# Sliding-window attention feeding an FFN: scores packed into full PSUM banks across units, sink scores of four units in one column-tiled group

## The chip, the cores and the metric

The kernel runs on one core of one Trainium2 chip. The metric is the device time of one execution in microseconds (us). Of the kernel before there are three runs: 232.1, 232.37 and 232.55 us, median 232.37.

## The reference

```python
batch, n_heads, seq, head_dim = (4, 8, 768, 64)
n_sink, window = (4, 128)
n_tokens, d_model, d_ff = (3072, 512, 2048)

def _attn_ref(q, k, v, n_sink, window):
    scale = 1.0 / np.sqrt(D)
    scores = scale * np.matmul(q, k.transpose(0, 1, 3, 2))
    is_sink = pos[None, :] < int(n_sink)
    rel = pos[:, None] - pos[None, :]
    in_window = (rel >= 0) & (rel < int(window))
    scores = np.where(is_sink | in_window, scores, -1000000000.0)
    a = softmax(scores)
    return np.matmul(a, v)

def _moe_ref(x, w_in, w_out, beta):
    h = x @ w_in
    g = h * (1.0 / (1.0 + np.exp(-beta * h)))
    return g @ w_out
```

The attention output, transposed to tokens by 512 (heads x 64), is the x of the feed-forward part. Inputs and output are float32. A query sees the 128 keys of its window and the first 4 keys of its sequence, the sinks. In blocks of 128 that is its own block (the diagonal, "d"), the block before (the upper part, "p"), and for queries from block 2 on the four sinks as well. Query blocks 0 and 1 contain or touch the sinks in key block 0 ("s").

## The kernel before, in words

**Units.** The work of attention is cut into 32 units: a batch (4), half of its sequence (384 queries), and a pair of heads. Unit u is batch u // 8, half u // 4 % 2, pair u % 4. Four units make a half batch, called hb in the code (0 to 7), even ones the first half of a sequence, odd ones the second. The FFN runs on the same 384 tokens of a half batch, T_.

**Stages.** Each is a small function that records its operations in a graph (`Graph.add`):

- `load`, `cast`: q, k, v from HBM (SP queue) into float32 staging and then to bf16. v goes to `vaug` with a column of ones, which yields the softmax denominator.
- `T` (units of hb 0 to 2) and `XP` (later ones): transposed q and k, `qkT`, head pair in the 128 partitions, 64 each. `T` does it on TensorE, `XP` by DMA.
- `SC` (L609 to L653): scores of one unit, keys in the partitions. Each head uses 64 rows of the array. It takes four neighbouring PSUM banks of 512 float32 columns: two groups of blocks (`GROUPS`, L597), and for each group one bank a head. The first half of a sequence has groups of 3 and 2 blocks, the second half 3 and 3, so banks are filled to 384 or 256 columns of 512. An exponential on ACT for each group (L639) writes `E`, and GpSimd masks the "d" and "p" blocks (L645); the "s" blocks are multiplied by `maskS` (L651).
- `SS` (L655 to L667): sink scores of one unit. `kS` holds the 4 sink keys of each head, zero elsewhere, in columns 0 to 3 and 32 to 35 of 128. One matmul of 128x128 weights (L662) and one exponential (L665) into `ES`. `first_keys` (L550) fills `kS`, and two copies from `vaug` (L543) fill `vS`, the sink values.
- `AV` (L681 to L711): for each of three query blocks the sink product (L691, one matmul for both heads) and the window products (L701); then a reciprocal and a multiplication on VectorE (L705, L707) give `onorm`.
- `OT`: `onorm` transposed to `xT`, on TensorE (L727) for the first units, later by DMA.
- `HQ` (L745): 4 matmuls of 384 columns for one of 16 chunks of the hidden layer; tanh on ACT (L750) and one VectorE operation (L752) give `g`. `OQ` (L765): 4 matmuls of 512 columns, one of four parts of a 128-token output; after the fourth it is copied and stored.

**What sets the order.** The main loop at the end of `_program` keeps a planned clock, and at each step takes the first stage, in the order OT, AV, SC, SS, T and then alternately HQ and OQ, whose inputs and PSUM banks are ready by the plan (`head`, L796). The attention of later half batches is so spread among the FFN of earlier ones. `Graph.arrange` then orders all operations again, with planned durations, may swap neighbouring groups of TensorE, and chooses ACT, VectorE or GpSimd for copies that any of them can do. `resolve` sets the semaphore waits. Banks are taken with `take(n)`: n neighbouring banks that come free first. Up to 18 us matmuls on constants (L935) fill the gaps of TensorE.

Rings that bound how far stages run ahead: `NE` = 4 units of `E` and `ES`, `NKS` = 4 of `kS`, `NON` = 5 of `onorm`, `NTT` = 3 of the tanh output.

Of the kernel before, what the change touches and what calls it, by code (L numbers as in the profile page):

```python
# [347 lines left out]
def _program(nc, G, sb, ps, q, k, v, w_in, w_out, beta, out):  # L348
    NU = 2 * NPAIR
    NSTG, NX, NV, NT, NE, NON, NG, NTT, NOS, NKS, NWS = 2, 2, 3, 12, 4, 5, 3, 3, 4, 4, 6  # L350
# [22 lines left out]
    E = sb("E", (128, 6, 2, 128), BF16, NE)  # L373
    ES = sb("ES", (128, HALF), BF16, NE)
    kS = sb("kS", (128, 128), BF16, NKS)
    vS = sb("vS", (128, H, D + 1), BF16, 2)
    onorm = sb("onorm", (128, NK, 2, D), BF16, NON)
# [45 lines left out]
    def banks_at(n):  # L423
        c = choose(n)
        return c and c[0]
# [23 lines left out]
    def consts():  # L449
# [11 lines left out]
        for i in range(NKS):  # L461
            add("gp", lambda e, i=i: e.memset(kS[i][:, :], 0.0), 80, w=[("kS", i)])
        for i in range(2):
            add("gp", lambda e, i=i: e.memset(vS[i][:, :, :], 0.0), 350, w=[("vS", i)])
# [54 lines left out]
    def cast(hb, n, i):  # L519
# [18 lines left out]
        if n == "v" and hb % 2 == 0 and i == 0:  # L538
            z = hb // 2 % 2
            v0 = vaug[hb % NV][0:NSINK, 0, :, :].rearrange("p (a two) d -> p a two d", two=2)  # L540
            for hh in range(2):
                dst_ = vS[z][32 * hh:32 * hh + NSINK, :, :].rearrange("p (a two) d -> p a two d", two=2)[:, :, hh, :]
                add("dve", lambda e, dst_=dst_, hh=hh: e.tensor_copy(dst_, v0[:, :, hh, :]), 200,  # L543
                    r=[("vS", z), ("v", hb % NV, 0)], w=[("vSd", z, hh)])
# [5 lines left out]
    def first_keys(u):  # L550

        ks = u % NKS
        kd = kS[ks][:, :].rearrange("p (a w) -> p a w", w=32)[:, 0:2, 0:NSINK]
        add("gp", lambda e: e.tensor_tensor(
            kd, qkT[:, u % NT, 1:2, 0:NSINK].to_broadcast([128, 2, NSINK]),
            headm[:, :].unsqueeze(2).to_broadcast([128, 2, NSINK]), ALU.mult), 200,
            r=[("kS", ks), ("qkT", u % NT, 1, 0), "headm0", "headm"], w=[("kSd", ks)])

    def XP(hb, n, c):
# [9 lines left out]
        if hb % 2 == 0 and (n, c) == ("k", 0):  # L569
            for j in range(4):  # L570
                first_keys(4 * hb + j)

    def T(u):
# [16 lines left out]
        if hb % 2 == 0:  # L590
            first_keys(u)
# [5 lines left out]
    GROUPS = [[[("s", 0, 0), ("s", 0, 1), ("d", 1, 1)], [("d", 2, 2), ("p", 1, 2)]],  # L597
              [[("d", 3, 3), ("p", 2, 3), ("p", 3, 4)], [("d", 4, 4), ("d", 5, 5), ("p", 4, 5)]]]

    def slots(half):  # L600

        out_, i = {}, 0
        for j, grp in enumerate(GROUPS[half]):
            for blk in grp:
                out_[blk] = (j, i)
                i += 1
        return out_

    def SC(u):  # L609
        G.begin()  # L610
        b, half, hp = where(u)
        z = u % NE
        bs = take(4)
        for j, grp in enumerate(GROUPS[half]):

            jobs = {}
            for i, (kind, kb, qb) in enumerate(grp):
                jobs.setdefault(kb, []).append((qb, i))
            for kb, cols in jobs.items():
                cols.sort()  # L620
                own = u if kb >= NK * half else u - 4
                kt = qkT[:, own % NT, 1, :]
# [3 lines left out]
                for hh in range(2):  # L626
# [3 lines left out]
                    add("pe", lambda e, dst=dst, kt=kt, kc=kc, rows=rows, q0=q0, nq=nq: e.matmul(  # L630
                        dst, kt[rows, kc:kc + 128],
                        qkT[rows, u % NT, 0, q0:q0 + 128 * nq].rearrange("p (s w) -> p s w", w=128),
                        start=True, stop=True), mm_ns(128 * nq) / 2 + 24,
                        r=qk_keys(u) + (qk_keys(own) if own != u else []), x=[("B", bs[2 * j + hh])])
        for j, grp in enumerate(GROUPS[half]):
            n, s0 = len(grp), slots(half)[grp[0]][1]
            src = P[:, bs[2 * j]:bs[2 * j] + 2, 0:128 * n].rearrange("p h (s w) -> p h s w", w=128)
            dst_ = E[z][:, s0:s0 + n, :, :].rearrange("p s h w -> p h s w")
            add("act", lambda e, src=src, dst_=dst_: e.activation(dst_, src, AF.Exp, bias=0.0, scale=SCALE),  # L639
                act_ns(256 * n), w=[(k_, z, j) for k_ in "Edps"], x=[("B", i) for i in bs[2 * j:2 * j + 2]])  # L640
            for kind, sg in (("d", 1), ("p", -1)):
                at_ = [i for i, blk in enumerate(grp) if blk[0] == kind]
                if at_:
                    d = E[z][:, s0 + at_[0]:s0 + at_[-1] + 1, :, :].rearrange("p s h w -> p (s h) w")
                    add("gp", lambda e, d=d, sg=sg, at_=at_: e.affine_select(  # L645
                        d, d, [[0, 2 * len(at_)], [sg, 128]], ALU.is_ge, 0.0, base=min(sg, 0), channel_multiplier=-sg),
                        pool_ns(256 * len(at_), 2 * len(at_)), r=[("E", z, j)], w=[(kind, z, j)])
            if grp[0][0] == "s":
                d = E[z][:, s0:s0 + 2, :, :]
                mask = maskS[:, :, :].unsqueeze(2).to_broadcast([128, 2, 2, 128])  # L650
                fn = lambda e, d=d, mask=mask: e.tensor_tensor(d, d, mask, ALU.mult)  # L651
                any_of({"gp": (fn, 1150), "dve": (fn, 335)}, r=[("E", z, j), "maskS"], w=[("s", z, j)])
        give(bs)  # L653

    def SS(u):  # L655

        G.begin()
        b, half, hp = where(u)
        z, ks = u % NE, (u - 4 * half) % NKS
        q0 = 0 if half else 256  # L660
        bs = take(1)
        add("pe", lambda e: e.matmul(P[:, bs[0], q0:HALF], kS[ks][:, :], qkT[:, u % NT, 0, q0:HALF], start=True,  # L662
                                     stop=True), mm_ns(HALF - q0),
            r=[("kSd", ks)] + qk_keys(u), x=[("B", bs[0])])
        add("act", lambda e: e.activation(ES[z][:, q0:HALF], P[:, bs[0], q0:HALF], AF.Exp, bias=0.0, scale=SCALE),  # L665
            act_ns(HALF - q0), w=[("ES", z)], x=[("B", bs[0])])
        give(bs)  # L667

    def parts(half):

        sl = slots(half)
        return [[(blk[0], sl[blk][0], sl[blk][1], blk[1])
                 for blk in sorted(sl, key=lambda x: "spd".index(x[0])) if blk[2] == qb]
                for qb in range(NK * half, NK * half + NK)]

    def av_keys(u):
        z = u % NE
        ks = {(p[0], z, p[1]) for ps in parts(where(u)[1]) for p in ps}
        return sorted(ks) + [("v", u // 4 % NV, c) for c in range(NK)] + [("ES", z), ("vSd", u // 8 % 2, 1)]

    def AV(u):  # L681
        G.begin()
        b, half, hp = where(u)
        z, on = u % NE, u % NON
        bs = take(1)
        A = P[:, bs[0], :]
        for m, ps in enumerate(parts(half)):
            far = NK * half + m >= 2
            if far:
                c0 = 2 * m * (D + 1)  # L690
# [105 lines left out]
    def head(s):  # L796
# [10 lines left out]
        elif s in ("SC", "SS"):  # L807
            if i >= NU or i >= done["AV"] + NE:
                return None
# [192 lines left out]
```

The softmax here doesn't subtract the row's maximum and nothing guards it: scores larger than these inputs give would overflow.

## Time and profile before

| | |
|---|---|
| time, median of three | 232.37 us |
| span of the profiled execution | 230.6 us |
| TensorE (PE) busy | 216.6 us, 94% |
| ScalarE (ACT) busy | 156.6 us, 68% |
| VectorE (DVE) busy | 135.0 us, 59% |
| GpSimd (POOL) busy | 73.3 us, 32% |
| DMA queue of the loads and stores | 72.7% of 16 engines' span |

How to read the profile: section 2 of its page cuts the span into 40 slices of 5.77 us, a digit is the busy share in tenths. A row of a group gives line, engine, operation, output and inputs, shapes, count, then busy us and mean ns of one, then the idle time of the engine before it and what ended it. A row of the timeline gives start, duration, engine, line, operation and how many; the durations of matmuls overlap, so the distance of two starts says how long PE was held. PEld is the weight load.

### The profile page before, as it was taken

What the parts mean: (1) busy time and instruction counts of PE and PEld (TensorE: products, weight loads), DVE (VectorE), ACT (ScalarE), POOL (GpSimd) and SP (SyncE); (2) the same over time, 40 slices, a digit from 0 to 9 for tenths busy, and PEclk for the clock granted to TensorE, in tenths of its full rate; (3) what the DMA queues carried; (4) which work ended last, traced back from release to release, by engine and by line L of the source; (5) the groups of instructions that cost most, each with busy time, mean ns of one, the idle gap of its engine ahead of it and who ended that gap; (6) DMA issues with size and microseconds to landing.
All of it is one profiled execution on the core that took longest, in us unless ns stands there. A gap on an engine that the chain in (4) does not pass through costs nothing.

```text
span 230.6 us, 4557 instructions
## 1 busy us (share of the span) xinstructions
PE 216.6 (94%) x1730; PEld 122.0 (53%) x1756; DVE 135.0 (59%) x285; ACT 156.6 (68%) x282; POOL 73.3 (32%) x163
## 2 busy tenths in 40 slices
PE   7986899899999999999998999999999999999993
PEld 5563555356555555555554455645554665555541
DVE  3895698987783567747574554836665453633310
ACT  2867979487882986686777776867769754744431
POOL 6583953022361572153001493225002730000000
PEclk9999999999999999999999999999999999999999
DMA  5999999999859988899439979997587022011112
GB/s 159 249 325 261 296 388 387 356 247 223 128 126 241 209 113 163 216 189 162 92 96 251 218 106 204 259 170 134 87 185 219 20 80 64 3 45 45 45 50 89
DMA packets 94997, 39.76 MB, mean 172 GB/s; under 512 B 81648, under 2 KB 87808, under 8 KB 94976
## 3 DMA queue, kind: packets, MB, share of 16 engines
q1 hardware_dynamic: 94976, 39.47, 72.7%
q8 instruction: 14, 0.23, 0.4%
q14 instruction: 7, 0.06, 0.1%
HBM read 27.27 MB, written 6.29 MB: 146 GB/s over the span
## 4 chain that ended last, share of the span: by engine, by line
PE 76%; DMA 10%; ACT 4%; SPq 4%; DVE 2%; issue 1%; POOL 1%
PE P L765 34%; PE P L745 30%; DMA wst<-in_moe_w_in_dram 4%; PE P L630 4%; DMA k_stage<-in_k_dram 4%; SPq L499 4%; PE P L701 4%; DMA v_stage<-in_v_dram 2%; DVE g L752 1%; ACT t L750 1%; PE P L691 1%; ACT qkT L439 1%; ACT E L639 1%; PE P L662 1%; PE P L581 1%
## 5 line engine op out<-in xcount | busy, mean ns | idle before, releaser
L752 DVE SCALAR_TENSOR_TENSOR g<-t,P 128x384 bf16<-128x384 f32 x128 | 69.6, 552 | 49.3 <-ACT t L750 45.6
L750 ACT ACTIVATE t<-P,hbeta 128x384 f32<-128x384 f32 x128 | 73.6, 588 | 35.0 <-PE P L745 28.6
L745 PE MATMUL P<-xT,w_in 128*128 128x384 bf16 x512 | 96.3, 326 | 0.9 <-DVE w_in L444 0.3
L765 PE MATMUL P<-w_out,g 128*128 128x512 bf16 x358 | 91.8, 379 | 2.7 <-DVE g L752 1.3
L645 POOL TENSOR_SCALAR_AFFINE_SELECT E<-E 128x512 bf16<-128x512 bf16 (+1 forms) x112 | 55.2, 522 | 66.7 <-ACT E L639 66.1
L745 PEld LDWEIGHTS P<-xT,w_in 128*128 128x128 bf16 x512 | 48.1, 98 | 37.6 <-DVE g L752 0.9
L765 PEld LDWEIGHTS P<-w_out,g 128*128 128x128 bf16 x384 | 35.6, 98 | 37.1 <-DVE g L752 2.8
L639 ACT ACTIVATE E<-P 128x768 bf16<-128x768 f32 x64 | 45.6, 770 | 7.5 <-PE P L630 7.3
L439 ACT ACTIVATE osb<-P 128x512 f32<-128x512 f32 x20 | 12.0, 599 | 12.7 <-PE P L765 11.2
L701 PE MATMUL P<-vaug,E 128*128 128x65 bf16 x352 | 18.9, 193 | 0.7 <-DVE vaug L444 0.7
L701 PEld LDWEIGHTS P<-vaug,E 128*128 128x128 bf16 x352 | 16.7, 97 | 4.2 <-DVE vaug L444 0.9
L707 DVE TENSOR_TENSOR onorm<-P,rden 128x384 bf16<-128x384 f32 x32 | 17.8, 557 | 1.0
L630 PE MATMUL P<-qkT 64*128 64x128 bf16 (+1 forms) x256 | 16.1, 239 | 1.0 <-ACT E L639 0.9
L630 PEld LDWEIGHTS P<-qkT 64*128 64x128 bf16 x256 | 8.6, 94 | 11.3 <-issue 5.0
L444 DVE CAST q<-q_stage 128x512 bf16<-128x512 f32 (+1 forms) x17 | 9.0, 540 | 7.0 <-DMA q_stage<-in_q_dram 7.0
L691 PE MATMUL P<-vS,ES 128*128 128x130 bf16 x64 | 12.8, 220 | 0.0
L444 DVE CAST vaug<-v_stage 128x512 bf16<-128x512 f32 x16 | 7.3, 456 | 8.2 <-DMA v_stage<-in_v_dram 8.1
L665 ACT ACTIVATE ES<-P 128x128 bf16<-128x128 f32 (+1 forms) x32 | 10.9, 410 | 0.4 <-PE P L662 0.4
L441 POOL TENSOR_SCALAR_AFFINE_SELECT vaug<-v_stage 128x512 bf16<-128x512 f32 x3 | 2.1, 693 | 25.5 <-DMA v_stage<-in_v_dram 25.5
L651 DVE TENSOR_TENSOR E<-E,maskS 128x512 bf16<-128x512 bf16 x15 | 7.0, 463 | 5.0 <-ACT E L639 4.8
L444 DVE CAST k<-k_stage 128x512 bf16<-128x512 f32 (+1 forms) x14 | 6.5, 464 | 5.7 <-DMA k_stage<-in_k_dram 5.5
L935 PE MATMUL P<-ones 128*128 128x256 bf16 x47 | 8.7, 322 | 1.1 <-POOL ones L450 1.1
(50 smaller groups left out, 107.1 us busy)
## 6 DMA issues: line engine op xcount, KB each, us to landing
v_stage<-in_v_dram SPq DMA_DIRECT2D x24, 256.0 KB, 4.6
out_dram<-osb SPq DMA_DIRECT2D x24, 256.0 KB, 2.4
q_stage<-in_q_dram SPq DMA_DIRECT2D x15, 256.0 KB, 4.9
k_stage<-in_k_dram SPq DMA_DIRECT2D x15, 256.0 KB, 4.9
wst<-in_moe_w_in_dram SPq DMA_DIRECT2D x5, 512.0 KB, 9.1
wst<-in_moe_w_out_dram SPq DMA_DIRECT2D x4, 512.0 KB, 6.8
g<-in_moe_w_out_dram SPq DMA_DIRECT2D x4, 512.0 KB, 7.1
q_stage<-in_q_dram SPq DMA_DIRECT2D x2, 768.0 KB, 7.2
```

What stands on the lines that cost most here:

```text
L439: return lambda e: e.activation(dst, src, AF.Copy, bias=0.0, scale=scale)
L444: return lambda e: e.tensor_copy(dst, src)
L630: add("pe", lambda e, dst=dst, kt=kt, kc=kc, rows=rows, q0=q0, nq=nq: e.matmul(dst, kt[rows, kc:kc + 128], qkT[rows, u % NT, 0, q0:q0 + 12 ...
L639: add("act", lambda e, src=src, dst_=dst_: e.activation(dst_, src, AF.Exp, bias=0.0, scale=SCALE), act_ns(256 * n), w=[(k_, z, j) for k_ i ...
L645: add("gp", lambda e, d=d, sg=sg, at_=at_: e.affine_select(d, d, [[0, 2 * len(at_)], [sg, 128]], ALU.is_ge, 0.0, base=min(sg, 0), channel_ ...
L691: add("pe", lambda e, m=m, c0=c0: e.matmul(A[:, c0:c0 + 2 * (D + 1)], ES[z][:, m * 128:(m + 1) * 128], vS[b % 2][:, 2 * hp:2 * hp + 2, :]. ...
L701: e.matmul(A[:, c0:c0 + D + 1], E[z][:, i, hh, :], vaug[vz][:, kb % NK, 2 * hp + hh, :], start=a, stop=o, skip_group_check=True), 39,
L707: add("dve", lambda e: e.tensor_tensor(onorm[on][:, :, :, :].rearrange("p m h d -> p (m h) d"), av[:, :, 0:D], rden[on][:, :].unsqueeze(2) ...
L745: add("pe", lambda e, c=c: e.matmul(hp, w_in16[:, c, m * 128:(m + 1) * 128], xT[:, c, t0:t0 + HALF], start=(c == 0), stop=(c == 3)), mm_ns ...
L750: add("act", lambda e: e.activation(tt[ti][:, :], hp, AF.Tanh, bias=0.0, scale=hbeta[:, m:m + 1]), act_ns(HALF) + 93, r=["hbeta"], w=[("t" ...
L752: add("dve", lambda e: e.scalar_tensor_tensor(gt[T_ % NG][:, m, :], tt[ti][:, :], 1.0, hp, ALU.add, ALU.mult), dve_ns(HALF), r=[("t", ti)] ...
L765: add("pe", lambda e, m=m: e.matmul(P[:, bk, :], gt[T_ % NG][:, m, t * 128:(t + 1) * 128], w_out16[:, m, :], start=(m == 0), stop=(m == NM ...
```

## The change

It repacks the scores and merges the sink scores.

- **Tiles instead of groups.** `tiles_of` lists tiles of exactly four blocks, each in one bank a head, so 512 of 512 columns. In an even half batch each unit fills one tile with s, s, d, d, and the four "p" blocks of the four units share a fifth tile. In an odd half batch two units share three tiles. `E` becomes a ring of 7 tiles, and blocks that a later AV needs are found through `PLACE`.
- **Bursts.** `SC(n)` now does burst n: two tiles (one in half batch 0), four banks at once. There are three bursts for each half batch after the first (six a batch, for eight before).
- **Sinks in one group.** `SS` is no stage of its own. It runs inside the last burst of an even half batch and inside the first of an odd one, for the four units together: four matmuls of 32 weight columns, each to 32 partitions of the same bank, and one exponential. `kS` keeps the four units side by side, 32 columns each.
- **Sink values by DMA.** `vS` must now hold head h in partitions 16 h to 16 h + 3. Four small DMAs (`load_first`) bring the first four values of all batches and heads into `vS32`, and one VectorE multiplication a batch by a 0/1 table `own` spreads them (`first_values`), in place of the two copies.
- **Masks.** All masks on GpSimd are of two blocks and two heads, 512 columns.
- The planner's conditions follow: scores of a unit are counted as done when the last burst that holds a block of it is done (`units_scored`).

The core of the diff:

```diff
-    NSTG, NX, NV, NT, NE, NON, NG, NTT, NOS, NKS, NWS = 2, 2, 3, 12, 4, 5, 3, 3, 4, 4, 6
+    NSTG, NX, NV, NT, NE, NON, NG, NTT, NOS, NWS = 2, 2, 3, 12, 7, 5, 3, 3, 4, 6
...
-    E = sb("E", (128, 6, 2, 128), BF16, NE)
-    ES = sb("ES", (128, HALF), BF16, NE)
-    kS = sb("kS", (128, 128), BF16, NKS)
+    E = sb("E", (128, 4, 2, 128), BF16, NE)
+    ES = sb("ES", (128, HALF), BF16, 2)
+    kS = sb("kS", (128, 128), BF16, 2)
...
+    def load_first(s_):
+
+        add("sp", lambda e: e.dma_start(vS32[s_:128:16, :, :], v[:, :, s_, :].rearrange("b h d -> h b d")), 60,
+            r=["vS32z"], w=[("vS32", s_)], dma=f"ds{s_}")
+
+    def first_values(b):
+
+        z = b % 2
+        add("dve", lambda e: e.tensor_tensor(
+            vS[z][:, :, 0:D], vS32[:, b:b + 1, :].to_broadcast([128, H, D]),
+            own[:, :].unsqueeze(2).to_broadcast([128, H, D]), ALU.mult), dve_ns(H * D),
+            r=[("vS32", s_) for s_ in range(NSINK)] + ["own", ("vSo", z)], w=[("vS", z)])
...
-    GROUPS = [[[("s", 0, 0), ("s", 0, 1), ("d", 1, 1)], [("d", 2, 2), ("p", 1, 2)]],
-              [[("d", 3, 3), ("p", 2, 3), ("p", 3, 4)], [("d", 4, 4), ("d", 5, 5), ("p", 4, 5)]]]
...
+    def tiles_of(hb):
+
+        u = 4 * hb
+        if hb % 2 == 0:
+            return [[("s", u + i, 0, 0), ("s", u + i, 0, 1), ("d", u + i, 1, 1), ("d", u + i, 2, 2)]
+                    for i in range(4)] + [[("p", u + i, 1, 2) for i in range(4)]]
+        out_ = []
+        for a in (u, u + 2):
+            b_ = a + 1
+            out_ += [[("d", a, 3, 3), ("d", a, 4, 4), ("p", a, 2, 3), ("p", a, 3, 4)],
+                     [("d", a, 5, 5), ("d", b_, 3, 3), ("p", a, 4, 5), ("p", b_, 2, 3)],
+                     [("d", b_, 4, 4), ("d", b_, 5, 5), ("p", b_, 3, 4), ("p", b_, 4, 5)]]
         return out_
...
+        step = 1 if hb_ == 0 else 2
+        runs_ = [list(range(i, min(i + step, first + n_))) for i in range(first, first + n_, step)]
+        with_first = len(runs_) - 1 if hb_ % 2 == 0 else 0
+        BURSTS += [(r_, hb_ if i == with_first else None) for i, r_ in enumerate(runs_)]
...
+    def SC(n):
         G.begin()
-        b, half, hp = where(u)
-        z = u % NE
-        bs = take(4)
-        for j, grp in enumerate(GROUPS[half]):
+        tiles, first = BURSTS[n]
+        bs = take(2 * len(tiles))
+        f_ = take(1) if first is not None else None
+        for j, t_ in enumerate(tiles):
...
+        if first is not None:
+            SS(first, f_[0])
...
-                act_ns(256 * n), w=[(k_, z, j) for k_ in "Edps"], x=[("B", i) for i in bs[2 * j:2 * j + 2]])
...
+                act_ns(1024), w=[("E", z)] + [("m", z, i) for i in range(4)],
+                x=[("B", i) for i in bs[2 * j:2 * j + 2]])
...
-        add("pe", lambda e: e.matmul(P[:, bs[0], q0:HALF], kS[ks][:, :], qkT[:, u % NT, 0, q0:HALF], start=True,
-                                     stop=True), mm_ns(HALF - q0),
-            r=[("kSd", ks)] + qk_keys(u), x=[("B", bs[0])])
...
+    def SS(hb, bank):
+
+        ks, z = hb // 2 % 2, hb % 2
+        q0 = 0 if hb % 2 else 256
+        for j in range(4):
+            u = 4 * hb + j
+            add("pe", lambda e, j=j, u=u: e.matmul(
+                P[32 * j:32 * j + 32, bank, q0:HALF], kS[ks][:, 32 * j:32 * j + 32], qkT[:, u % NT, 0, q0:HALF],
+                start=True, stop=True), 100 if j == 0 else (mm_ns(HALF - q0) if j == 3 else 5),
+                r=[("kSd", ks, j)] + qk_keys(u), x=[("B", bank)])
+        add("act", lambda e: e.activation(ES[z][:, q0:HALF], P[:, bank, q0:HALF], AF.Exp, bias=0.0, scale=SCALE),
+            act_ns(HALF - q0), w=[("ES", z)], x=[("B", bank)])
...
+            if first is not None and first >= 2 and done["AV"] < 4 * (first - 1):
+                return None
```

## The prediction

> **What bounds the kernel now.** I read the page's header first, then the busy rows by slice, then the chain that ended last.
>
> ```profile
> span 230.6 us, 4557 instructions
> PE 216.6 (94%) x1730; PEld 122.0 (53%) x1756; DVE 135.0 (59%) x285; ACT 156.6 (68%) x282; POOL 73.3 (32%) x163
> PE   7986899899999999999998999999999999999993
> DVE  3895698987783567747574554836665453633310
> DMA  5999999999859988899439979997587022011112
> PE 76%; DMA 10%; ACT 4%; SPq 4%; DVE 2%; issue 1%; POOL 1%
> ```
>
> PE carries 76% of the chain and its row is nearly all nines from the eighth slice (about 41 us) on, so there a microsecond of PE work removed is a microsecond of span. Before that it is not full: DMA is saturated and DVE stands at 8 or 9. So I treat two stages apart: the start (to 43.75 us) and the steady part (43.75 to 218.83 us, where the last run of output matmuls begins).
>
> Next the groups by shape, for the operations that the change touches (PE, ACT and POOL answers one after the other).
>
> ```profile
> L630 PE MATMUL P<-qkT 64*128 64x256 bf16 x96 | 12.1, 277 | 0.9 <-ACT E L639 0.9
> L630 PE MATMUL P<-qkT 64*128 64x128 bf16 x160 | 12.0, 216 | 0.1
> L662 PE MATMUL P<-qkT,kS 128*128 128x384 bf16 x16 | 3.8, 329 | 0.2 <-ACT qkT L439 0.2
> L662 PE MATMUL P<-qkT,kS 128*128 128x128 bf16 x16 | 2.6, 221 | 0.0
> L639 ACT ACTIVATE E<-P 128x768 bf16<-128x768 f32 x48 | 37.8, 823 | 7.5 <-PE P L630 7.3
> L639 ACT ACTIVATE E<-P 128x512 bf16<-128x512 f32 x16 | 9.7, 609 | 0.0
> L665 ACT ACTIVATE ES<-P 128x384 bf16<-128x384 f32 x16 | 6.9, 520 | 0.4 <-PE P L662 0.4
> L665 ACT ACTIVATE ES<-P 128x128 bf16<-128x128 f32 x16 | 3.9, 299 | 0.0
> L645 POOL TENSOR_SCALAR_AFFINE_SELECT E<-E 128x256 bf16<-128x256 bf16 x80 | 35.7, 462 | 26.1 <-ACT E L639 25.6
> L645 POOL TENSOR_SCALAR_AFFINE_SELECT E<-E 128x512 bf16<-128x512 bf16 x32 | 21.5, 673 | 40.6 <-ACT E L639 40.5
> ```
>
> PE durations include pipeline latency and overlap, so they are no price. The price is the distance from one start to the next in the timeline of PE:
>
> ```profile
> 58.40 1.03 PE L765 MATMUL P<-w_out,g 128*128 128x512 bf16 x4
> 59.36 0.45 PE L630 MATMUL P<-qkT 64*128 64x256 bf16 x8
> 59.74 0.82 PE L745 MATMUL P<-xT,w_in 128*128 128x384 bf16 x4
> ...
> 83.31 1.03 PE L765 MATMUL P<-w_out,g 128*128 128x512 bf16 x4
> 84.27 0.50 PE L630 MATMUL P<-qkT 64*128 64x256 bf16 x8
> 84.71 0.82 PE L745 MATMUL P<-xT,w_in 128*128 128x384 bf16 x4
> ...
> 96.18 0.39 PE L662 MATMUL P<-qkT,kS 128*128 128x128 bf16 x4
> 96.40 0.81 PE L765 MATMUL P<-w_out,g 128*128 128x512 bf16 x3
> ...
> 120.47 0.81 PE L662 MATMUL P<-qkT,kS 128*128 128x384 bf16 x4
> ```
>
> Four 512-wide matmuls in a row take 0.865 us. So the scores at 59.36 begin 0.095 us later than 58.40 + 0.865: an entry cost. A first-half unit then holds PE 0.38 us, a second-half unit (84.27 to 84.71) 0.44 us. These are 5 and 6 blocks of 128 columns for each head. Sixteen 384-wide FFN matmuls in a row take 2.60 us (0.1625 each), so a block of 128 columns takes 0.054 us: 5 blocks are 0.27 us if the two heads run side by side, and 0.54 if not. So they do run side by side, and 0.11 us is left over as exit, in both kinds (6 blocks: 0.325). A score burst costs its blocks x 0.054 + 0.21. Four sink matmuls cost 0.22 us (128 wide, 96.18 to 96.40) and 0.65 us (384 wide, to the next start at 121.12).
>
> **The skill.** "TensorEngine Tiling (Array Packing)", Key Properties: changing the tiling mode drains TensorE. My 0.21 us around each 64-row burst agrees. Its Restrictions: column tiling turns off fast weight load. No run here shows it. "TensorE: Matmul & The Clock Gate", Measured speedup vs the span model: three column tiles side by side gave 2.38 times, and a pack lasts about one matmul plus a few ns a tile. The trace has no column tile; its row pairs agree in kind. "ScalarE: Activation LUTs", What ACT_TABLE_LOAD costs: 186 ns + 0.833 ns an element with immediate operands, and neighbours overlap by 93 ns. The trace agrees: 823 at 768 (826 by that), 609 at 512 (613). So a 1024-wide exponential is estimated at 1.04 us, 0.95 back to back.
>
> **The change, part by part.**
>
> Scores. Before: 16 x (0.38 + 0.095) + 16 x (0.44 + 0.095) = 16.2 us. After, the column count is the same, but in bursts of 8 blocks a head (4 for the last burst of an even half batch): half batch 0 keeps single tiles, 5 bursts, 20 x 0.054 + 5 x 0.21 = 2.1 us; the three other even ones 1.08 + 3 x 0.21 = 1.7 each; the four odd ones 1.29 + 3 x 0.21 = 1.9 each. Sum 14.8. In odd half batches blocks that shared keys are split over tiles: 40 matmuls for 32, so 32 more in all. They add no columns; an extra weight load is at most 0.03 us (in the AV runs 11 matmuls pass in 0.37 us), so 0 to 1.0 us; I take half. Half batch 0 lies in the start and even loses 0.2, so the steady gain is 1.6 - 0.5 = 1.1 us.
>
> Sinks. Before: 4 x (0.22 + 0.65) = 3.5 us. After: 8 groups of four 32-column matmuls. Side by side: 4 x (0.054 + 0.162) = 0.86 us, plus one more mode change each. Bounds for that change: nothing, or 0.2 us (as a score burst pays). I take 0.2: 2.5 us in all, gain 1.0. If the four ran one after another it would be 3.5 + 1.6 = 5.1, a loss of 1.6; with no change cost the gain is 2.6.
>
> ACT. 64 exponentials become 44 of the same total width: 20 x (0.19 - 0.09) = 2 us. 32 sink exponentials (10.8 us) become 8 (16 x 0.52 and 16 x 0.30 fall to 4 each: 2.7), saving 8 us. ACT is 68% busy and PE hides it in the steady part: worth nothing there. POOL: 112 masks (57.2 us) become 72 of 512 (72 x 0.673 = 48.5). Hidden too. DVE: eight 0.26 us copies become four multiplies of 512 elements, unseen here; nearest is L707 (0.557 for 384), so about 0.7, bounds 0.56 to 0.8; +0.7 us, hidden behind a DVE that is half idle, except at the start.
>
> New waits. In an even half batch no AV can start before the last burst (p tile and sinks of all four units), its exponential and two masks (0.95 + 1.35). In the order of the changed program's instructions (fixed when it is built, so it can be read without running it) 16 output matmuls (3.5 us) stand between that burst and the AVs in the second and fourth batch, 8 (1.7 us, so up to 0.6 is open) in the third: hidden but for that. A burst needs 4 banks in a row plus one; queued behind a stuck burst on PE would be the FFN matmuls.
>
> The start. Four tiny loads go in on the SP queue after the first v loads. The 8 KB beta load shows 0.5 us of issue, so 2 us. Behind them wait q and k of half batch 1. But k was issued at 9.99 us and needed 8.84 to land, DMA being full, so the delay stays in the backlog. The sink values land late, about 14.5 us; AV of unit 0 stood at 12.65 and really waited for v until 13.8. The last transposed output was at 17.98, and T of half batch 1 waited for k until 19.3 anyway. So 1 us there is free. After that all six tiles of half batch 1 come before the first FFN matmul: ACT needs 6 x 0.95 + 0.45 after 22.2, and the third burst waits for banks until about 24.6, so FFN starts about 25.3 instead of 24.18: a loss of 1.1. Then PE no longer meets the two late score units (26.12, 34.87) and the late output of unit 7 (idle 1.04 us at 41.79). Work to 43.75 was 19.4 us in 25.6, 6.2 idle. By my count of the changed order the same work ends about 2.1 us earlier if only PE and ACT count; but DVE, full in 28 to 34 and 36 to 44, gets two more 0.7 us weight casts there. That leaves 0 to 2.1; I take 1.0.
>
> Sum: 1.1 + 1.0 + 1.0 = 3.1, so 229.2.
>
> **Rivals.**
> - The start gives all of its 2.1 us and the column groups change mode for little: 232.4 - 2.1 - 2.2 - 1.3 = 226.8. For it: ACT loses 10 us of work and the page's DVE row is the only other full one. Against: DVE.
> - Small gain: column tiles drain more than I think, or the start gives nothing: 231.3 (the 1.1 of scores alone).
> - Slower. Sink tiles run one by one (+1.6), scores gain only 0.6, coupling four units puts waits of some 0.3 us before AV in seven half batches (+2): 232.4 + 1.6 - 0.6 + 2 = 235.4 at the worst, 233.5 when half of the waits come. For it: a late tile now holds four units, and the plan's durations are not the chip's. Against: the steady part has little waiting now (it is some 4 us above its work, 2.4 of that entries).
>
> **Chances.** 229.2: 0.58. 226.8: 0.17. 231.3: 0.10. 233.5: 0.15. The range from 226.3 to 232.2 takes in the second and third case and leaves out the slow one and a little below. Faster 0.81, same 0.04 (the small-gain case shrunk), slower 0.15.
>
> **What would show it.** Right: four sink matmuls take about 0.25 us (128 wide) and 0.36 (384 wide) of PE with their change, not 0.22 and 0.65 plus it; a two-tile burst takes about 0.64 with entry; the exponential of 1024 lasts 1.04 us; the first FFN matmul comes near 25.3 us, the first output matmul near 41; the tail from the last FFN matmul on is unchanged. Wrong: PE idle before AV or score bursts behind ACT or POOL in the steady part, k of half batch 1 landing 1 us later than 18.8, or DVE holding FFN groups up to 45 us.

## The result and the profile after

The changed kernel takes 229.08 us (median of 4 executions, 227.61 to 229.99) against 232.46 us before on the same chip: a ratio of 0.9845, with a 95% interval of 0.9802 to 0.9887. The forecast was 229.2 us. In four profiled executions of the changed kernel (this one and runs 1, 5 and 11) the stretch from the last transposes of queries and keys to the last run of output matmuls is the same to 0.01 us; what differs between them lies ahead of it. The kernel before was profiled once.

The page of the changed kernel, the lines that answer to those of before:

```profile
span 225.7 us, 4586 instructions
PE 215.4 (95%) x1795; PEld 123.8 (55%) x1795; DVE 139.5 (62%) x293; ACT 142.5 (63%) x226; POOL 64.8 (29%) x118
PE   8977799998999999999999999999999999999993
DVE  2796399996665556577875653958756554533310
DMA  6979999999949995959348995959849223011112
PE 85%; DVE 4%; ACT 4%; DMA 2%; SPq 2%; issue 1%; POOL 1%
```

PE's share of the chain rose from 76% to 85%, and DMA's fell from 10% to 2%. That is no measure of the gain: most of the 10% lies in the first 34 us, where the chain of before runs through the landing of a key load and of a weight load (8.84 and 9.89 us) and the chain of the changed kernel takes another way. The slices from 11 to 28 us (7, 7, 7) are where PE still waits.

The groups by shape (instructions, busy us, mean ns):

```profile
L690 ACT ACTIVATE E<-P 128x1024 bf16<-128x1024 f32 x44 | 43.0, 1032 | 10.2 <-PE P L678 9.9
L720 ACT ACTIVATE ES<-P 128x384 bf16<-128x384 f32 x4 | 2.0, 503 | 0.0
L720 ACT ACTIVATE ES<-P 128x128 bf16<-128x128 f32 x4 | 1.1, 284 | 0.0
L703 POOL TENSOR_SCALAR_AFFINE_SELECT E<-E 128x512 bf16<-128x512 bf16 x72 | 48.6, 702 | 78.6 <-ACT E L690 78.2
L560 DVE TENSOR_TENSOR vS<-vS,own 128x512 bf16<-128x512 f32 x4 | 3.6, 909 | 0.2 <-PE P L746 0.2
```

The exponential of 1024 elements has its estimated size (1.032 us for 1.04). The multiply that fills the sink values does not: 0.91 us, not 0.7. ScalarE lost 14.1 us of busy time, GpSimd 8.5, and VectorE gained 4.5.

The timeline of PE in the steady part. The distance from a start to the next is the price:

```profile
56.43 1.03 PE L821 MATMUL P<-w_out,g 128*128 128x512 bf16 x4
57.39 0.62 PE L678 MATMUL P<-qkT 64*128 64x256 bf16 x12
57.94 0.82 PE L801 MATMUL P<-xT,w_in 128*128 128x384 bf16 x4
...
63.23 0.40 PE L678 MATMUL P<-qkT 64*128 64x128 bf16 x8
63.56 0.24 PE L716 MATMUL P<-qkT,kS 128*32 128x128 bf16 x4
63.73 1.47 PE L821 MATMUL P<-w_out,g 128*128 128x512 bf16 x6
...
76.70 0.62 PE L678 MATMUL P<-qkT 64*128 64x256 bf16 x14
77.25 0.35 PE L716 MATMUL P<-qkT,kS 128*32 128x384 bf16 x4
77.53 0.82 PE L801 MATMUL P<-xT,w_in 128*128 128x384 bf16 x4
...
214.00 7.93 PE L821 MATMUL P<-w_out,g 128*128 128x512 bf16 x36
```

A two-tile burst enters at 56.43 + 0.865 + 0.095 = 57.39 and holds PE 0.55 us, whether it has 12 matmuls (57.39 to 57.94) or 14 (76.70 to 77.25). A single tile holds it 0.33. Per tile that is 0.22 = 4 x 0.054, with the same 0.11 left for the exit as before. Four column-tiled sink matmuls of 128 columns take 0.17 us and of 384 columns 0.28. Side by side they need 0.054 and 0.162, so their mode change costs about 0.12.

**Where the time came from.** Both programs have the same last transposes of queries and keys on PE (units 8 to 11). From their end up to the last run of output matmuls, PE does FFN, scores, sinks, attention and a few transposed outputs. Before: 56.01 to 218.83, 162.82 us. After: 55.78 to 214.00, 158.22. The changed order has by then done four FFN matmuls more, 0.65 us. The ends of the stretch, before and then after (the last line after stands above):

```profile
56.01 0.81 PE L745 MATMUL P<-xT,w_in 128*128 128x384 bf16 x4
218.83 7.93 PE L765 MATMUL P<-w_out,g 128*128 128x512 bf16 x35
```

```profile
55.78 0.81 PE L801 MATMUL P<-xT,w_in 128*128 128x384 bf16 x4
```

So the steady stretch gave 162.82 - 158.22 - 0.65 = 3.95 us, and the start 56.01 - 55.78 + 0.65 = 0.88. After the last run begins, nothing changed (11.8 and 11.7 us). Of the 3.95 us, 3.6 can be assigned:
- scores of six half batches: before 12 x 0.475 + 12 x 0.535 = 12.12; after 3 x (2 x 0.645 + 0.425) + 3 x 3 x 0.645 = 10.95: 1.17, and 0.1 more because one burst follows another directly at 101.4 us and spares an entry
- sinks of three batches: before 3 x 0.87 = 2.61; after 3 x 0.45 = 1.35: 1.26
- two waits of PE for VectorE that the changed order doesn't have, at 97.60 and 125.40, 0.55 and 1.03 us by their starts: 1.58; less two small waits of its own, about 0.15 in the transposed outputs at 69.8 and 0.33 for a mask at 104.64: 1.1.

The scores and the sinks are less work for PE; the third part is less waiting. It is read from a single trace of the kernel before, so how far these waits differ between its executions is not known.

The larger of these waits in the kernel before, in VectorE's timeline and then in PE's:

```profile
118.47 2.50 DVE L752 SCALAR_TENSOR_TENSOR g<-t,P 128x384 bf16<-128x384 f32 x4 [0.96 <-ACT t L750]
123.27 0.43 DVE L444 CAST vaug<-v_stage 128x512 bf16<-128x512 f32 x1 [2.29 <-DMA v_stage<-in_v_dram]
124.45 0.43 DVE L444 CAST vaug<-v_stage 128x512 bf16<-128x512 f32 x1 [0.74 <-DMA v_stage<-in_v_dram]
124.79 1.48 DVE L752 SCALAR_TENSOR_TENSOR g<-t,P 128x384 bf16<-128x384 f32 x3
```

```profile
123.94 0.59 PE L765 MATMUL P<-w_out,g 128*128 128x512 bf16 x2
125.40 0.39 PE L765 MATMUL P<-w_out,g 128*128 128x512 bf16 x1 [0.86 <-DVE g L752]
```

Two value casts stand ahead of the FFN's g in VectorE's order of instructions, and their loads land late: VectorE idles 2.29 and 0.74 us for them, and g follows only then, at 124.79. In the changed order the casts come elsewhere. No part of the change aims at this.

### The profile page after: what moved, and what is told of

Its sections match the earlier page's. It is cut to its first block, busy times and chain, and to the rows that moved or that the text cites. A ratio compares the mean times of both kernels' runs of the same rounds, so it can differ in the third digit from the quotient of the medians.

```text
span 225.7 us, 4586 instructions
## 1 busy us (share of the span) xinstructions
PE 215.4 (95%) x1795; PEld 123.8 (55%) x1795; DVE 139.5 (62%) x293; ACT 142.5 (63%) x226; POOL 64.8 (29%) x118
## 4 chain that ended last, share of the span: by engine, by line
PE 85%; DVE 4%; ACT 4%; DMA 2%; SPq 2%; issue 1%; POOL 1%
PE P L801 38%; PE P L821 36%; PE P L757 4%; PE P L678 4%; DMA k_stage<-in_k_dram 2%; ACT E L690 2%; PE P L746 2%; SPq L510 1%; DVE onorm L763 1%; ACT qkT L444 1%; DVE vS L560 1%; PE P L602 1%; PE P L783 1%; POOL E L703 1%; DVE E L698 1%
## 5 line engine op out<-in xcount | busy, mean ns | idle before, releaser
L821 PE MATMUL P<-w_out,g 128*128 128x512 bf16 x384 | 94.9, 379 | 0.0
L703 POOL TENSOR_SCALAR_AFFINE_SELECT E<-E 128x512 bf16<-128x512 bf16 x72 | 48.6, 702 | 78.6 <-ACT E L690 78.2
L690 ACT ACTIVATE E<-P 128x1024 bf16<-128x1024 f32 x44 | 43.0, 1032 | 10.2 <-PE P L678 9.9
L444 ACT ACTIVATE osb<-P 128x512 f32<-128x512 f32 x19 | 11.4, 600 | 20.1 <-PE P L821 19.9
L757 PE MATMUL P<-vaug,E 128*128 128x65 bf16 x352 | 17.2, 193 | 0.2 <-POOL E L703 0.2
L678 PE MATMUL P<-qkT 64*128 64x128 bf16 (+1 forms) x288 | 14.5, 230 | 0.9 <-ACT ES L720 0.6
L449 DVE CAST k<-k_stage 128x512 bf16<-128x512 f32 (+1 forms) x19 | 10.0, 532 | 3.7 <-DMA k_stage<-in_k_dram 3.7
L761 DVE RECIPROCAL rden<-P 128x6 f32<-128x6 f32 x32 | 6.0, 189 | 9.5 <-PE P L757 9.5
L449 DVE CAST vaug<-v_stage 128x512 bf16<-128x512 f32 x21 | 10.0, 479 | 3.1 <-DMA v_stage<-in_v_dram 3.0
L446 POOL TENSOR_SCALAR_AFFINE_SELECT q<-q_stage 128x512 bf16<-128x512 f32 x6 | 4.5, 755 | 24.4 <-DMA q_stage<-in_q_dram 24.4
L698 DVE TENSOR_TENSOR E<-E,maskS 128x512 bf16<-128x512 bf16 x16 | 9.1, 580 | 2.3 <-ACT E L690 2.1
L444 ACT ACTIVATE qkT<-P 128x768 bf16<-128x768 bf16 x9 | 6.9, 812 | 5.0 <-PE P L602 5.0
```

The source lines that it names most:

```text
L444: return lambda e: e.activation(dst, src, AF.Copy, bias=0.0, scale=scale)
L449: return lambda e: e.tensor_copy(dst, src)
L703: add("gp", lambda e, dd=dd, sg=sg: e.affine_select(dd, dd, [[0, 4], [sg, 128]], ALU.is_ge, 0.0, base=min(sg, 0), channel_multiplier=-sg), ...
L757: e.matmul(A[:, c0:c0 + D + 1], E[t_ % NE][:, i, hh, :], vaug[vz][:, kb % NK, 2 * hp + hh, :], start=a, stop=o, skip_group_check=True), 31,
L821: add("pe", lambda e, m=m: e.matmul(P[:, bk, :], gt[T_ % NG][:, m, t * 128:(t + 1) * 128], w_out16[:, m, :], start=(m == 0), stop=(m == NM ...
```

## The experiments

Runs 1 to 4, 5 to 8, 9 to 11, and 12 each shared a chip and the runs of the kernel before: 233.14, 232.74, 233.41 and 232.87 us there. In five of the fourteen profiles (runs 3, 4, 5, 6 and 12, five different kernels) the granted TensorE clock fell to 0.50 for 3.4 us, in run 12 twice, which costs an execution about 2 us (last section); so I weigh stretches of the traces above medians of a few executions.

**1. The changed kernel again.** No edit.

> The changed kernel, nothing edited, to get a second profile and a tighter time. Theory (a fixed amount of TensorE work is gone, the rest is the start and how late the DMAs land there): median 228 to 230 us, the steady part from the transposes of half batch 2 (end at 55.8 us in the first profile) to the last output run (214.0) again 158.2 us within 0.5, any difference between executions lies before 60 us or in waits for v loads. Rival (the runs differ because the chip's TensorE clock differs): the steady part itself is longer by 1 to 2 us with the same order and no waits.

228.63 us, ratio 0.980 (0.9747 to 0.9854). The steady stretch is 56.49 to 214.72: 158.23 us, the 158.22 of the first profile. The start gave only 56.01 - 56.49 + 0.65 = 0.17. So the steady gain is a property of the program and the start's gain is not.

**2. Sink matmuls at full width.**

```diff
-  P[32 * j:32 * j + 32, bank, q0:HALF], kS[ks][:, 32 * j:32 * j + 32], ...
+  P[:, bank, q0:HALF], kS[ks][:, :], ...
-  r=[("kSd", ks, j)] + qk_keys(u)
+  r=[("kSd", ks, i) for i in range(4)] + qk_keys(u)
```

> The four sink matmuls of a group use all 128 weight columns and write the whole bank one after another, so no column tile is left; the order of all engines is that of the changed kernel. The sink scores are then those of the last unit's queries for all four units, so that part of the output changes. Theory (column tiles run side by side and cost one mode change): each group takes 0.22 us instead of 0.17 (128 wide) and 0.65 instead of 0.28 (384 wide), 4 x 0.05 + 4 x 0.37 = 1.7 us, of which the groups of half batch 0 and 1 may hide in the start: 1.2 to 1.7 us slower than the changed kernel. Rival (the mode change costs as much as the tiles save): within 0.3 us of it.

229.57 us, 0.9 more than run 1, with intervals that overlap (0.9773 to 0.9865 for run 2); the traces decide. The two kinds of group in PE's timeline:

```profile
64.94 0.40 PE L716 MATMUL P<-qkT,kS 128*128 128x128 bf16 x4
65.18 1.03 PE L821 MATMUL P<-w_out,g 128*128 128x512 bf16 x4
...
78.68 0.82 PE L716 MATMUL P<-qkT,kS 128*128 128x384 bf16 x4
79.34 0.81 PE L801 MATMUL P<-xT,w_in 128*128 128x384 bf16 x4
```

0.24 and 0.66 us for 0.17 and 0.28: three batches lose 3 x (0.07 + 0.38) = 1.35 by that, and the steady stretch is 159.45, 1.22 longer. The column tiles do run side by side, and their mode change (about 0.12 us; at full width the group costs its columns and at most 0.02 more) is far smaller than what they save in the 384-wide group; in the 128-wide one it takes most of it back.

**3 and 4. Each half of the change alone.** Run 3 keeps the full banks and takes the sinks of before (one matmul, one exponential a unit); run 4 keeps the bursts of before and takes the sink groups with their loads. Both are planned anew.

```diff
# run 3, against the changed kernel
-        if first is not None:
-            SS(first, f_[0])
...
+    def SS(u):
...
+        add("pe", lambda e: e.matmul(P[:, bs[0], q0:HALF], kS[ks][:, :], ...
# run 4, against the kernel before
-    def SS(u):
+    def SS(hb):
...
+        for j in range(4):
...
+                P[32 * j:32 * j + 32, bank, q0:HALF], kS[ks][:, 32 * j:32 * j + 32], ...
```

> Only the packing of the scores (tiles, bursts); sinks for each unit as before, with 4 buffers of sink keys and 3 of sink exponentials. Theory (the parts add): scores gain 1.2 to 1.6 us of TensorE work plus what the start gives, so 230 to 231.2 us. Rival (the packing only pays together with the merged sinks because of the start and ACT): 232 or more.

> Only the merged sinks (one group of four column tiles for each half batch, a stage of its own, small loads, one multiplication for the sink values); scores for each unit as before. Theory: sinks gain 1.7 us of TensorE less up to 0.8 for eight mode entries of their own, so 230.7 to 231.5 us. Rival (ACT or the waits on four units decide): within 0.3 us of the kernel before, or slower.

Run 3 gained 0.6 us (ratio 0.9964, 0.9935 to 0.9992) and run 4 2.0 (0.9913, 0.9884 to 0.9942); together 2.6, where both in one gain 4.5. Run 4 lies in its theory's range. Run 3 does not: 232.56 us is the rival's number. Its trace gives another reason than the rival's, a wait of its own order in PE's timeline:

```profile
161.71 0.81 PE L784 MATMUL P<-xT,w_in 128*128 128x384 bf16 x4
164.57 0.62 PE L660 MATMUL P<-qkT 64*128 64x256 bf16 x14 [2.04 <-DMA qkT<-k]
```

A burst asks for transposed keys that SyncE issued late (the last piece at 162.03), and PE stands for 2.04 us. Then the granted clock is 0.50 from 165.8 to 169.2 us, up to 1.7 us more in this execution. So the halves cannot be added up by these runs: each new order draws its own waits, as the kernel before had drawn 1.58 us. Nothing here shows that the halves need each other, and nothing excludes it.

The start of run 3 tells something else. It has no small loads: its DMA engines stay full (busy share 1.00 and 1.08 at 10 to 14 us), VectorE's first cast of the second half batch's keys starts at 18.05 us, the first FFN matmul at 24.17, and by the reckoning above its start gave 56.01 - 55.41 + 0.65 = 1.25 us. Runs 7 and 10 come back to this.

**5 and 6. Late sink values.** Run 5 is the changed kernel once more. In run 6 the multiply of a batch waits for its own value cast:

```diff
-  r=[("vS32", s_) for s_ in range(NSINK)] + ["own", ("vSo", z)], w=[("vS", z)])
+  r=[("vS32", s_) for s_ in range(NSINK)] + ["own", ("vSo", z), ("v", 2 * b % NV, 0)], w=[("vS", z)])
```

> The changed kernel unaltered, on the chip and in the rounds of the next three, as their yardstick. Every theory expects 228.6 to 229.3 us and a ratio to the kernel before near 0.982.

> The multiply that fills the sink values of a batch (L560) waits for that batch's own value cast, so VectorE does only one of them in the start, not two in a row; TensorE, ScalarE and SyncE keep their instructions and order. Theory A (the start is set by the landing of the second half batch's keys, at 19.3 to 19.7 us, and VectorE's chain through the four normalised outputs has slack behind it): no difference from the changed kernel, within 0.3 us. Theory B (the second multiply, 0.85 us, delays the outputs, their transposes and ScalarE's key cast behind them): faster by 0.5 to 0.85 us.

229.39 and 230.38 us, with intervals that overlap (0.9817 to 0.9895, 0.9828 to 0.9922). The medians cannot tell 0 from 0.85 us. In the traces, which both have the clock's fall, the first FFN matmul comes at 26.55 and 26.52, and the steady stretch is 158.23 in both. That is theory A: taking the second multiply out of the start changes nothing there.

**7 and 10. Small loads on ScalarE's queue**, with the edit of run 6. The planner's order of the first 15 us shifts by a few instructions with it. Run 11 is the changed kernel again.

```diff
-  add("sp", lambda e: e.dma_start(vS32[s_:128:16, :, :], ...
+  add("act", lambda e: e.dma_start(vS32[s_:128:16, :, :], ...
```

> As the run before, and the four small sink-value loads are issued by ScalarE at 2.3 to 5 us, where it idles, rather than by SyncE at 9.4 to 12.1 us ahead of the second half batch's queries and keys (the planner's order in the first 15 us shifts by a few instructions with it). Theory A (SyncE's 2.7 us of issuing is what lets the DMA engines run dry and puts the keys late): the mean DMA share at 10 to 14 us is back at 1.0 or more from 0.77 and 0.34 to 0.47, the keys land 0.5 to 0.9 us earlier, FFN matmuls start as much earlier, and the time falls by 0.5 to 1.0 us against the changed kernel. Theory B (the prediction's: the issuing stays in the backlog, and the keys land when the bytes ahead of them have gone through): within 0.3 us.

> The version with the small loads on ScalarE's queue and late sink values once more, beside the changed kernel in the same rounds. If its gain is the start's (FFN 0.2 to 0.45 us earlier): faster than the changed kernel by 0.2 to 0.8 us. If the 1.8 us of its first run were of the start's lower TensorE clock, which is granted now and then to any of these kernels: within 0.3 us.

> The changed kernel unaltered, the yardstick of the two before. 228.6 to 229.4 us; where the granted clock falls at the first FFN matmuls (25 to 30 us), 2.0 to 2.5 us more in that execution.

227.60 us against 229.39 for run 5, and 228.10 against 229.05 for run 11: ratios to before of 0.9788 (0.9749 to 0.9827) and 0.9791 (0.9751 to 0.9832). In both pairs it has the lower median, by 1.8 and 0.95 us, more than was expected; the intervals still overlap (run 5: 0.9817 to 0.9895, run 11: 0.9803 to 0.9861). SyncE's issues in run 11, the changed kernel, and in run 10:

```profile
5.35 3.94 SPq L510 DMA_DIRECT2D v_stage<-in_v_dram  x3
9.34 2.69 SPq L554 DMA_DIRECT2D vS<-in_v_dram  x4
12.07 0.45 SPq L510 DMA_DIRECT2D q_stage<-in_q_dram  x1
12.57 1.57 SPq L510 DMA_DIRECT2D k_stage<-in_k_dram  x1
```

```profile
5.84 3.51 SPq L510 DMA_DIRECT2D v_stage<-in_v_dram  x3
9.40 0.93 SPq L510 DMA_DIRECT2D q_stage<-in_q_dram  x1
10.37 1.12 SPq L510 DMA_DIRECT2D k_stage<-in_k_dram  x1
```

Four loads of 8 KB hold SyncE for 2.69 us. Behind them the keys are issued at 12.57, not 10.37. What the DMA engines do meanwhile is in the windows (the last two columns are their busy share and GB/s), first run 11, then run 10:

```profile
10.00:12.00 2.00, 2.00 (x28) 1.25 (x27) 1.73 (x4) 1.99 (x4) 1.53 (x3) 1.00 0.92 174
12.00:14.00 2.00, 1.95 (x25) 1.52 (x25) 1.89 (x4) 1.98 (x3) 2.00 (x4) 1.00 0.36 45
```

```profile
10.00:12.00 2.00, 1.46 (x20) 1.18 (x20) 2.00 (x5) 1.12 (x2) 0.66 (x2) 1.00 1.27 206
12.00:14.00 2.00, 1.82 (x28) 1.28 (x26) 2.00 (x5) 1.13 (x3) 0.97 (x2) 1.00 0.99 273
```

The engines run dry: 45 GB/s at 12 to 14 us. VectorE's first cast of those keys starts at 19.93 in run 11, waiting for them, and at 18.80 in run 10; the first FFN matmul follows at 26.60 and 25.42. In run 7 it was less: keys at 19.44, FFN at 26.11. By the reckoning of the first section the start gave 0.04 us in run 11, 0.75 in run 7 and 1.44 in run 10. In run 7 the three value loads held SyncE for 4.14 us, for 3.51 in run 10, the keys were issued at 11.07, and the DMA share at 10 to 14 us was 0.94 and 0.85. Run 7 alone lies within the scatter of the changed kernel, whose first profile has the FFN at 25.94. But in runs 1, 5, 6, 7, 10 and 11 and in that profile the first FFN matmul comes 6.6 to 6.8 us after the first cast of those keys, so a late landing is a late FFN. Theory A holds in kind; its size varies.

**8 and 12. ScalarE's saving given back.** Each exponential of 1024 elements is done in two, then in four pieces, in unchanged order.

```diff
-  e.activation(dst_, src, AF.Exp, bias=0.0, scale=SCALE)
+  for h in range(2):
+      for s_ in (slice(0, 2), slice(2, 4)):
+          i_ = e.activation(dst_[:, h, s_], src[:, h, s_], AF.Exp, bias=0.0, scale=SCALE)
```

> Each of the 44 exponentials of 1024 elements is done as two of 512, with the order of every engine kept. By the kernel before's own row (609 ns for 512 elements) ScalarE does 44 x (2 x 0.609 - 1.032) = 8.2 us more, which takes it above what the change saved it less 6. Theory A (TensorE sets the pace and ScalarE's saving is hidden behind it): slower than the changed kernel by 0 to 0.7 us, all of it before 30 us, where TensorE waits for exponentials. Theory B (part of the gain comes from the shorter exponentials): slower by 1.5 us or more, with new waits of TensorE on L690 in the steady part.

> Each of the 44 exponentials of 1024 elements is done as four of 256, every engine's order kept. The halves had made ScalarE busy for only 2.2 us more (144.7 for 142.5), since neighbours overlap; [...]132 more of them should add 7 to 12 us, about the 10 that the change saved ScalarE. Theory A (ScalarE's saving is hidden behind TensorE): 0.5 to 1.2 us slower than the changed kernel, all of it in the start, where FFN waits for the exponentials of the second half batch (27 to 27.5 us for 26 to 26.6), and from there to the last run of output matmuls still 188.2 us, within 0.5. Theory B (the saving is part of the gain): 190 us or more for that stretch, with waits of TensorE on exponentials or on masks behind them.

The halves made ScalarE busy for 144.7 us, not for the 8.2 more that I expected: neighbours overlap, so durations of single instructions don't add up. That run (229.77 us; steady stretch 158.29) told little by itself. The quarters took it to 150.1, 7.6 more than the changed kernel, about half of what the change saved ScalarE: 231.03 us (0.9858 to 0.9942). Its profile has the clock's fall twice, from 20.9 and from 27.8 us on. From the first FFN matmul to the last output run it is 190.3 us, which by the number is theory B; but 1.7 us of the excess (31.74 for 30.02 in run 11) lie ahead of the end of the last transposes, around the second fall. After that, the steady stretch is 158.60, 0.38 longer, most of it around one wait, which the changed kernel has at half the length:

```profile
108.34 0.48 PE L762 MATMUL P<-vaug,E 128*128 128x65 bf16 x10 [0.30 <-POOL E L708]
```

So this half of ScalarE's saving is hidden in the steady part: theory A there. What it is worth in the start is not shown. The first FFN matmul came 0.9 to 1.5 us later (27.46), but the clock was 0.50 from 20.9 to 24.3, in the transposes ahead of it; from the first exponential of the second half batch to the first FFN matmul it is 3.87 us for 3.32 in run 11, so some 0.55 us can be the exponentials'. No run gives GpSimd its saving back.

**9. Single-tile bursts.**

```diff
-        step = 1 if hb_ == 0 else 2
+        step = 1
```

> Every burst of scores holds one tile, not two: full banks, the same matmuls, exponentials and sinks, but 18 more bursts (5 for 3 in three even half batches, 6 for 3 in four odd ones). Theory A (the scores' gain is the cost of entering and leaving the 64-row mode, 0.096 us in and 0.11 us out, paid less often): 18 x 0.205 = 3.7 us more of TensorE, slower than the changed kernel by 3 to 4 us and so back near the time of before; a single-tile burst holds TensorE 0.33 us with 0.096 ahead of it. Theory B (the gain comes from fewer instructions on ScalarE and GpSimd, and TensorE takes small bursts as well as large ones): within 1 us of the changed kernel.

234.03 us (ratio 1.0007, 0.9981 to 1.0033): 5.0 more than run 11, so the whole gain is gone, more than theory A's 3 to 4 us. The sum behind theory A was wrong, though. The new order put many single tiles back to back, where no mode changes, as at 79.49 in PE's timeline (12 matmuls in one stay of 0.55 us):

```profile
79.49 0.62 PE L678 MATMUL P<-qkT 64*128 64x256 bf16 x12
80.04 1.04 PE L821 MATMUL P<-w_out,g 128*128 128x512 bf16 x4
81.01 0.40 PE L678 MATMUL P<-qkT 64*128 64x128 bf16 x8
81.34 0.39 PE L821 MATMUL P<-w_out,g 128*128 128x512 bf16 x1
...
175.72 0.40 PE L678 MATMUL P<-qkT 64*128 64x256 bf16 x6 [1.68 <-DMA qkT<-k]
```

From the first FFN matmul on, PE takes up scores 23 times, not 17: 6 x 0.205 = 1.2 us at the most. Waits that the changed order doesn't have (0.82, 0.83, 1.68 and 0.29 us, at 148.5, 150.3, 175.7 and 177.2) make 3.6. The price of a burst stands; it is not shown that smaller bursts must lose that much.

## Why the forecast was right

The total was right to 0.1 us; its terms were not, and their errors cancelled. That it came so near is luck: the three other comparisons on a common chip gave a gain of 4.5, 3.4 and 4.4 us for the forecast's 3.1, and the spans of the two first profiles differ by 4.9.

- **Scores (gain 1.1, with 0.5 taken off for the 32 extra matmuls).** Mechanism right, the 0.5 taken off wrong. 14 matmuls in two tiles take the same 0.55 us as 12: the extra weight loads cost nothing. At the measured prices the seven half batches after the first gained 14.3 - 12.9 = 1.4 us (7 x 4 units at 0.475 or 0.535 before; 1.715 and 1.935 a half batch after), 1.17 of it past the last transposes, or 1.27 with the spared entry.
- **Sinks (gain 1.0, with 0.2 us for each mode change).** Mechanism right. The groups take 0.17 and 0.28 us, not 0.25 and 0.36, so four batches cost 1.8 us for 3.5 before: a gain of 1.7. Run 2 shows that column tiling carries it. The skill's note that a change of tiling mode drains TensorE ("TensorEngine Tiling (Array Packing)", Key Properties) agrees in kind: 0.12 us for a sink group, 0.21 for a score burst. Its pack of about one matmul plus a few ns a tile ("TensorE: Matmul & The Clock Gate", Measured speedup vs the span model) agrees once this change is taken off: 0.28 us for four of 162 ns, so 0.16 without it.
- **The start (gain 1.0).** FFN began at 25.94 us for the forecast's 25.3, the first output matmul at 41.14 for 41. The gain was 0.88 us in the first profile, 0.17 and 0.04 in runs 1 and 11; in run 5, with the clock's fall, it was a loss of 2.0. The step that failed is the sentence that 2 us of issue for the four small loads "stays in the backlog". They take 2.7 to 3 us, the queue runs dry, and the keys land at 19.3 to 19.9, not 18.8; runs 7 and 10 give 0.75 and 1.44 us when the loads are issued elsewhere, and run 3, which has no such loads (and the old sinks), gives 1.25. The forecast listed a late landing among its signs of error, and it came. The rest of this term fits: from the first cast of those keys to the first FFN matmul it is 5.3 us before and 6.7 after, 1.3 more where 1.1 was forecast, and from there to the end of the last transposes the changed order wins back 2.5 to 2.65 us (31.84 before; 29.84 and 30.02 in the first profile and run 11, with four FFN matmuls more). The first sink matmul waited for its values until 15.03, where 14.5 was estimated; the keys came later still, and the second multiply alone cost nothing (run 6).
- **ScalarE, GpSimd and VectorE (nothing).** Right for ScalarE as far as was tried: giving 7.6 of its 14.1 us back moved the steady stretch by 0.38 (run 12). For GpSimd no run tests it. The sum for the sink exponentials had a slip: four of each size are 3.3 us by its own durations, not 2.7; measured are 3.1. The exponential has the size worked out from "ScalarE: Activation LUTs", What ACT_TABLE_LOAD costs. The multiply of sink values was mis-sized (0.91 us for 0.7), without effect.
- **New waits.** Almost none: about 0.15 us at 69.8 and 0.33 for a mask at 104.64, by their starts, and in the steady stretch no burst is stuck for banks. (The forecast's slow case with half of the waits comes to 234.4 by its own terms, not 233.5.)
- **Not foreseen.** 1.58 us of waits for g in the kernel before went away with the new order. The forecast's sums do not hold such luck of an order; in runs 3 and 9 it went the other way, by 2.0 and 3.6.

In all, a gain of 3.95 us in the steady stretch and, where the clock held, 0.04 to 0.88 in the start, where 2.1 and 1.0 were forecast. Medians of the changed kernel lie 3.4 to 4.5 us below those of before in the four comparisons on a common chip.

What stays open: why the new order has no wait for g, and whether the kernel before has it in every execution. A version with the old bursts and only the value casts moved was not tried.

## What to carry to other kernels

Where TensorE sets the pace, price a regrouping by the distance from start to start in its timeline: columns at full rate plus a fixed cost for each change of tiling mode; fewer and fuller bursts pay for that, and extra small matmuls inside a burst may be free. A tiny DMA is not free: ask what waits behind its issue in the same queue, and whether the engines run dry meanwhile; an engine that idles at that moment can issue it. A regrouping after which a planner orders everything anew also draws a new set of waits (here worth 1.6 to 3.6 us), so compare long stretches between the same two instructions, not only totals, before crediting the edit.

## What the runs showed of the hardware

- Four column tiles of 128 x 32 with 384 columns run together in 0.28 us, mode change included; the same four at full width take 0.66.
- Four loads of 8 x 4 x 64 f32 (8 KB each) hold SyncE's queue for 2.7 to 3 us, 0.59 to 1.04 each, where an 8 KB load of 16 rows takes 0.46. ScalarE issues them in about as long (1.21 and 1.90 us for one and three, at 1.8 to 4.9 us).
- A chain of exponentials overlaps: twice 0.62 us for 512 elements makes ScalarE busy for 0.05 us more than one of 1024 (2.2 us for 44), where the durations differ by 0.21.
- The granted TensorE clock fell to 0.50 for 3.4 us at a time: from 26.1, 26.4 and 26.4 us on in runs 4, 5 and 6, from 20.9 and 27.8 in run 12, and from 165.8 in run 3. The windows of run 5 (the third column from the end is the clock; the fall lasts from 26.4 to 29.8 us, so the second and third window also hold some time at full clock):

```profile
24.00:26.00 2.00, 1.06 (x24) 0.64 (x20) 1.09 (x2) 2.00 (x4) 1.66 (x3) 1.00 0.91 182
26.00:28.00 2.00, 1.48 (x7) 0.74 (x6) 0.55 (x2) 2.00 (x3) 2.00 (x4) 0.59 0.92 265
28.00:30.00 2.00, 2.00 (x21) 1.37 (x19) 0.00 (x0) 2.00 (x4) 2.00 (x4) 0.56 1.03 371
30.00:32.00 2.00, 2.00 (x30) 1.40 (x26) 1.83 (x4) 0.75 (x2) 2.00 (x4) 1.00 1.05 404
```

The first eight FFN matmuls take 2.74 us there, and 1.47 in run 11 of the same kernel. From the first FFN matmul to the end of the last transposes it is 32.15 us in run 5 and 30.02 in run 11: 2.1 us lost. That is nearly as much as the scatter between most executions of one kernel. In runs 4, 5 and 6 the fall began 0.1 to 1 us ahead of the first FFN matmul. In the 3.4 us ahead of each fall PE was busy for 1.4 to 2.1 us; but in run 11 it was busy for 1.9 of the 3.4 us up to 26.36 and kept its clock, and so did run 9 after its wait of 1.68. What sets it off was not found.
